# A new annealed emission order for an attention and gated-FFN kernel, with the rms factor of batches 4 and 5 moved to ScalarE

## The chip, the cores and the metric

The kernel runs on one core of a Trainium2 chip. The metric is the device time of one execution in microseconds (us). "Span" is the time from the first to the last instruction in the profile of one execution.

## What is computed

The inputs are q, k and v (8 batches, 8 heads, sequence 576, head dimension 64), g_norm (64), w_in (512 x 1024), conv_w (3 x 1024) and w_out (1024 x 512), all in float32.

```python
kv = einsum('bhsd,bhse->bhde', k, v)             # linear attention: no softmax
out = einsum('bhsd,bhde->bhse', q, kv)
rms = sqrt(mean(out * out, axis=-1) + 1e-06)
x = out / rms * g_norm                           # heads joined: (8, 576, 512)
h = maximum(x @ w_in, 0)                         # (8, 576, 1024)
c = conv_w[0] * h[s - 1] + conv_w[1] * h[s] + conv_w[2] * h[s + 1]
result = (h * sigmoid(c)) @ w_out                # (8, 576, 512)
```

## The kernel before

**Work.** The eight batches form five groups, (0), (1), (2, 3), (4, 5) and (6, 7), called g0 to g4. Each batch loads q, k and v as bf16 (`load`, L237, issued by GpSimd, 576 KB each; every name has two buffers, so the load of batch b waits until batch b - 2 has been read). TensorE makes kv (`kv_mm`, L378), transposes q (`tr_mm`, L428) and multiplies (`out_mm`, L351, tile `ot_ps`). ScalarE squares the product (`square`, L451), TensorE sums the squares (`ss_mm`, L505), and the factor 1 / rms comes in one of two ways. With `by_act`, ScalarE does Ln and Exp (`ln_exp`, L516 and L517), ahead of which L512 loads the table of these functions if a sigmoid ran last; the first sigmoid after it loads its own again (at L792 in this profile). Without it, `mean` (ScalarE, L521), `guess` (VectorE, L526) and `newton` (twelve GpSimd operations, L532 to L535) do the same. The factor is then spread over the partitions: g0 to g2 keep the product in SBUF (`keep`, L335) and spread with a matmul (`rb_mm`); g3 and g4 store the factor to DRAM (`scr`, L579) and read it back with eight broadcast transfers of 288 KB (`rb`, L585), both issued by SyncE in `scatter`, and form the product again (`out_again`). VectorE multiplies (`x_mul`, L640; `x_scale`, L646), which gives xT.

The FFN takes eight blocks of 128 features for each batch: `h_mm` (L744), relu (`h_out`, L755 on ScalarE or L757 on VectorE), the convolution with `tap` (L808), `edge` (GpSimd, L820) and `add` (L829, L831) on VectorE, or on TensorE for g0 (`conv_mm`, L783), sigmoid (L835, or L792 for g0), `gate` (L840), and `o_mm` (L696) for 128 rows of output at a time, `o_out` (L331 or L333) and `o_store` (SyncE, L710). The last 64 rows of two batches share one `tails_mm` (L883). `move` (L331 on ScalarE, L333 on VectorE) does all plain copies out of PSUM.

**Order.** No compiler schedules this. Every unit of work is an operation made by `plan.op`, numbered in the order of these calls. The list ORDER gives the order in which the operations are emitted, and so the order of each engine's own in-order queue. "101a" puts operation 101 on ScalarE, "20d" on VectorE, and "41*6" puts six fill matmuls, which compute nothing that is used, ahead of operation 41 to keep TensorE busy. Waits between engines follow from the data and from the buffers. The costs, `dma`, `lat` and `lead` that `plan.op` gets were used by a planner outside this file to find the list; at run time only the list counts.

Some numbers, in the list of before: 17, 34, 106, 208, 230, 368, 386, 522 and 540 are the kv products of batches 0 (in two parts) to 7. 205 and 206 load k and v of batch 3; 362 to 364 load k, v and q of batch 4, 365 to 367 of batch 5, 516 to 518 of batch 6, 519 to 521 of batch 7. 13 and 14 load the halves of w_in, 15 and 16 those of w_out. 404 sums the squares of g3, 405 to 407 are its `mean`, `guess` and `newton`, 408 its `scatter`, 410 its first `x_scale`; 558 to 562 are the same five for g4. 151 and 175 are the `edge` copies of g1, 291 and 323 those of g2. As g3 has one operation in place of three in the changed kernel, all numbers above 405 fall by two there: `ln_exp` of g3 is 405, its `scatter` 406, the loads of batches 6 and 7 are 514 to 519, their kv products 520 and 538.

The two ways to the factor, as they are put in the plan:

```python
if g.by_act:
    me = rs = plan.op("ACT", 0.97, ln_exp,
                      deps=[ss] + ([g.new_rs] if ts[0] else []))
...
else:
    me = plan.op("ACT", 0.5, mean, deps=[ss])
    g.new_rs = rs = plan.op("DVE", 0.3, guess, deps=[me])
    rs = plan.op("POOL", 11.5, newton, deps=[rs])
```

Of the kernel before, what the change touches and what calls it, by code (L numbers as in the profile page):

```python
# [25 lines left out]
def _patch_pnc_remap() -> None:  # L26
# [40 lines left out]

BY_ACT = (1, 1, 1, 0, 0)
Q_DMA = (0, 0, 0, 0, 0)
# [6 lines left out]
ORDER = """  # L76
    12 7 8 9 10 17*15 18d 19 29 105 20a 21*1 11 22 30d 31*1 23d 33a 34 35d 36 37a 24*1 25d 32 26*5
    28d 27 41*6 42 0 1 2 3 38 108*4 39 40d 113 43 45 109d 123 124a 4 103 44 104 114d 47 48 46 49 50
    106*2 107a 51*1 52 53 118 119a 110*2 54 112d 111 115 13 55 117a 204 56d 68 116 120 69a 122d 121
    14 225 125 210 126 64 211d 226d 127a 65a 5 59 60a 128 129 73 203 74d 66 67 215 202 77 78a 207 86  # L80
    87a 216a 130 131 132 70 133 71 134 135 136 208 209a 137 205 138 220 221d 75 76 79 80 212 214d
    222 232 233d 237 139 213 223 140a 242 82 238a 224d 83d 243a 6 147 72 217 218 219a 141 142a 143
    144a 149 247 364 370 371a 248a 169 84 85 206 81 374 375d 148 367 227 228 229a 230 88 89 170a 163
    231d 234 235 236a 249 250 90 164d 251d 378 379d 244 245 246d 239 240 363 388 362 145 146a 392
    389d 393d 366 151 400*2 252 57 253 58 150 152 156 401d 241d 61 382 383d 154 62 368 369a 167*4
    168a 155 153 165 166a 254 255 157 372 396 373 365 376 256 16 269 397a 270 386 267 268 377 387a
    261*2 262 63 380*4 381 15 394*3 395 175 259 260 402*2 403 390*3 391 398*2 171 174 384 385 399
    160 173 172 176 179 180 518 521 91 92a 93 158 177 178 100 101a 404 181 257 265 263 405 406 258
    264 266 159 183 161 97 98d 162 184 185 182 186 94 95a 516 517 277 271 542 524 275 102 543a 528
    525a 529a 199 272a 278a 276d 522 523a 273 274d 279 280a 281 200a 99 282a 287 288 289 285 286d  # L90
    407 283 284a 307 308a 532 533a 530 531 554 555a 315 316a 309 310a 305 306a 519 290 291 520 292
    296 294 293 295 297 550 551a 408 303 304a 319 534 535 540 541a 320 317 318a 322 311 312a 313
    314a 546 547d 321 323 324 328 526 552 527 553 548 536 537a 556 557 193 549 538 539 544 545 201
    409 194a 325 410 413 414 558 411 415 195 559 560 196 421 298 301 416 417 190 96 197a 299 191a
    326 192 300 412 422 418 327 329 187 188a 189 198 425 426a 423 424 433 330 419 420 302 434a 461
    333 462a 435 427 428d 436d 441 443 332 331 334 429 437 561 438a 430a 439 440a 431 432a 442 445
    459 469 470a 463 465 464a 466a 460a 471 457 458a 444 446 450 449 467 356 468a 472a 448 447 451
    562 357a 358 473 475 476 474 454 338 339a 340 477 478 480 479 482 344 345a 455 346 353 354a 355
    359 360a 567 563 481 571 335 564 572 568 452 453 336a 347 565 348a 569 575 483 484 485 486 349
    341 570 576 350 566 577 361 578 573 574 456 579 580a 605 487 587 488 627 628a 585 586a 590 606a  # L100
    342a 343 581 582a 583 584a 591 351a 607 608a 588 589 592 593 594 596 595 597 352 337 603 604a
    609 610a 615 492 611 493a 674 675a 494 601 498 499a 599 613 489 500 600 490a 491 631 632a 504
    633 598 629 614 612 616 618 620 617 619 621 623 602 634a 630a 653 654a 639 622 505a 506 501 635
    638 636 637 640 641 642 643 624 502a 625 651 652a 503 507 508a 644 645 647 626 649 648 509 665
    510 511a 512 513 666a 646 514a 515 657 655 656 658 660 689 659 661 662 495 650 667 668 669 670
    690a 691 671 663 664 496a 497 683 684a 685 686 677 676 678 679 680 672 673 681 682 687a 688 692
    693d 694 701 702a 703 707 708d 709 704 705d 706 698 699d 700 695 696a 697
"""
# [5 lines left out]
class Ring:  # L114


    def __init__(self, bufs):
        self.free = bufs
# [12 lines left out]
class Op:  # L131

    def __init__(self, at, group, engines, cost, fn, args, deps, need, dma, lat):
        self.at, self.group, self.engines, self.cost = at, group, engines, cost
        self.fn, self.args, self.dma, self.lat = fn, args, dma, lat
# [13 lines left out]
class Plan:  # L151
# [12 lines left out]

    def op(self, engines, cost, fn, *args, deps=(), need=(), dma=0.0, lat=0.0):
        engines = engines if isinstance(engines, tuple) else (engines,)
        cost = cost if isinstance(cost, tuple) else (cost,) * len(engines)
        o = Op(len(self.ops), self.group, engines, cost, fn, args, deps, need, dma, lat)
        self.ops.append(o)
        return o  # L170
# [18 lines left out]
def kernel(  # L189
# [112 lines left out]
    plan = Plan()  # L302
# [191 lines left out]
    def normalize(g, first, ts, sums):  # L494
# [58 lines left out]
        def x_view(bi, t):  # L553
# [4 lines left out]
                                deps=mine, need=g.need_rs)  # L558
        for sq in mine:
            Hold(ring("sq", 8), sq, [ss])  # L560
# [3 lines that stand above are left out]
            if ts[0] == 0:  # L564
                g.new_rs = rs
# [10 lines left out]
        if g.x_from == "dma":  # L576
            def scatter():
# [10 lines left out]

            g.scatter = sp = plan.op("SP", 8.3, scatter, deps=[rs], need=g.need_rb,
                                     dma=4.0 * g.G, lat=0.5)  # L590
            g.free_rs = [sp]
# [5 lines left out]
        else:  # L597
            sp = rs
# [72 lines left out]
    def ffn(g):  # L671
# [15 lines left out]
        for t0, n in units:  # L687
# [29 lines left out]
            cuts = 1 + (t0 + n - 1) // PS - t0 // PS  # L717
            so = plan.op("SP", 0.6 * cuts, o_store, deps=[ev], dma=0.65, lat=2.0)
            Hold(ONE, om, [ev])
# [153 lines left out]
    def tails(pair):  # L873
# [26 lines left out]
        st["op"] = ev = plan.op(EITHER, (0.6, 0.69), o_out, deps=[om])  # L900
        so = plan.op("SP", 1.2, o_store, deps=[ev], dma=0.65, lat=2.0)
        Hold(ONE, om, [ev])
# [59 lines left out]
    for half in range(2):  # L962
        loaded["w_in", half] = plan.op("POOL", 0.77, load_w_in, half, dma=2.7)
    w_out_done = [plan.op("POOL", 0.77, load_w_out, half, dma=2.75) for half in range(2)]

    for g in groups:
        g.by_act, g.by_dma, g.x_from, g.kv_twice = (c[g.n] for c in (BY_ACT, Q_DMA, X_FROM, KV_TWICE))
        for b in g.bs:
            for name, src in (("k", k), ("v", v), ("q", q)):
                if b > 0:  # L970
                    need = []
                    if b > 1:
                        w, wi = where[b - 2]
                        need = w.free_q[wi] if name == "q" else w.free_k[wi]
                    loaded[name, b, 0] = load_ops[name, b] = plan.op(
                        "POOL", 0.77, load, b, name, src, need=need, dma=2.95,
                        deps=[load_ops[name, b - 1]] if b > 1 else [])
# [54 lines left out]
```

## Time and profile before

The median of three runs is 214.91 us (214.76 to 218.9). The profiled execution took 213.96 us, its span is 212.2 us.

| engine | busy us | share of the span | instructions |
|---|---|---|---|
| PE (TensorE matmuls) | 187.7 | 88% | 1877 |
| PEld (weight loads) | 117.9 | 56% | 1877 |
| DVE (VectorE) | 153.5 | 72% | 283 |
| ACT (ScalarE) | 141.1 | 66% | 227 |
| POOL (GpSimd) | 50.5 | 24% | 73 |

| stretch, us | PE busy | DVE busy | ACT busy | POOL busy | clock of TensorE | GB/s |
|---|---|---|---|---|---|---|
| 40 to 50 | 9.97 | 7.25 | 8.92 | 3.80 | 1.00 | 152 |
| 70 to 80 | 10.00 | 9.63 | 9.20 | 6.04 | 1.00 | 151 |
| 80 to 90 | 6.68 | 3.38 | 3.92 | 7.95 | 0.94 | 184 |
| 90 to 100 | 10.00 | 6.05 | 6.74 | 0.91 | 0.89 | 213 |
| 100 to 110 | 3.66 | 5.56 | 2.96 | 0.00 | 0.79 | 167 |
| 110 to 120 | 9.31 | 5.67 | 7.83 | 0.22 | 0.87 | 2 |
| 140 to 150 | 10.00 | 9.72 | 6.97 | 0.86 | 1.00 | 216 |

A share of busy time averages over stretches with different limits, so the second table matters more than the first: in each stretch, ask which engine is full, and where none is, what they all wait for. In the trace, "waits" add up idle time of an engine by what ended it (engine, line, total us, times, longest). The "chain" goes back from the last instruction to what released it, again and again, and is printed in order of time (start, length, what, how many).

### The profile page before, as it was taken

How to read it: one execution, taken by the hardware profiler on the slowest of the kernel's cores; microseconds unless marked ns; L12 is line 12 of the kernel's file. 1: busy time of each engine (PE TensorE's matmuls, PEld its weight loads, DVE VectorE, ACT ScalarE, POOL GpSimd, SP SyncE). 2: the span in 40 equal slices, each digit the busy share in tenths (PEclk: the TensorE clock that was granted, in tenths of full speed). 3: DMA queues.
4: the chain of work that ended last, by engine and by line, in shares of the span. 5: the costliest groups of instructions: out<-in, count | busy, mean ns of one | idle time of the engine just before them, and what ended most of it. 6: DMA issues, size and time to landing. Idle time of an engine off the chain costs nothing.

```text
span 212.2 us, 4655 instructions
## 1 busy us (share of the span) xinstructions
PE 187.7 (88%) x1877; PEld 117.9 (56%) x1877; DVE 153.5 (72%) x283; ACT 141.1 (66%) x227; POOL 50.5 (24%) x73
## 2 busy tenths in 40 slices
PE   1988999999799999399259998999999999999992
PEld 1655567777575447277246446784446756654440
DVE  2047775778899995148904999999997999899430
ACT  2054679797898995257427898857688868896401
POOL 7714020205130649601000199401000000000000
PEclk9999999999999999889958999999999999999999
DMA  3999999999999599799920133089722243145654
GB/s 54 200 202 204 205 205 204 169 196 141 205 205 205 75 216 248 122 209 226 234 47 0 44 93 114 29 182 218 203 73 73 68 130 100 50 112 161 166 143 114
DMA packets 31593, 31.01 MB, mean 146 GB/s; under 512 B 2108, under 2 KB 26964, under 8 KB 31572
## 3 DMA queue, kind: packets, MB, share of 16 engines
q0 software_dynamic: 20976, 16.25, 50.5%
q1 hardware_dynamic: 10596, 14.47, 26.9%
q8 instruction: 14, 0.23, 0.4%
q14 instruction: 7, 0.06, 0.1%
HBM read 37.24 MB, written 9.73 MB: 221 GB/s over the span
## 4 chain that ended last, share of the span: by engine, by line
PE 55%; DMA 23%; DVE 11%; ACT 4%; issue 3%; POOL 2%; SPq 0%; DVEq 0%; ACTq 0%; POOLq 0%
PE h_ps L744 25%; PE o_ps L696 18%; DMA v_sb<-in_v_dram 13%; DMA k_sb<-in_k_dram 4%; DMA q_sb<-in_q_dram 4%; PE kv_ps L378 3%; DMA out_dram<-o_sb 3%; PE c_ps L783 2%; DVE xT L646 2%; PE qT_ps L428 2%; DVE o L335 2%; DVE conv L831 2%; PE ot_ps L351 2%; ACT sq L451 1%; DVE conv L829 1%
## 5 line engine op out<-in xcount | busy, mean ns | idle before, releaser
L744 PE MATMUL h_ps<-xT,w_in_sb 128*128 128x288 bf16 x512 | 69.6, 292 | 1.8 <-DVE o L335 0.7
L696 PE MATMUL o_ps<-w_out_sb,h 128*128 128x512 bf16 x272 | 61.2, 379 | 0.1
L744 PEld LDWEIGHTS <-w_in_sb 128*128 128x128 bf16 x512 | 50.0, 100 | 17.8 <-issue 3.0
L755 ACT ACTIVATE h<-h_ps 128x576 bf16<-128x576 f32 x55 | 34.9, 653 | 14.7 <-PE h_ps L744 13.2
L696 PEld LDWEIGHTS <-h 128*128 128x128 bf16 x272 | 26.0, 98 | 30.8 <-issue 1.5
L808 DVE TENSOR_SCALAR tap<-h,cw_rel 128x576 bf16<-128x576 bf16 (+1 forms) x80 | 31.7, 440 | 10.8 <-ACT h L755 9.9
L835 ACT ACTIVATE conv<-conv,cw_rel 128x576 bf16<-128x576 bf16 (+1 forms) x40 | 37.0, 959 | 1.9 <-DVE conv L831 1.9
L331 ACT ACTIVATE o_sb<-o_ps 128x512 f32<-128x512 f32 x31 | 18.5, 597 | 17.8 <-PE o_ps L696 12.8
L820 POOL COPY conv<-h 128x4 bf16<-128x4 bf16 (+3 forms) x12 | 3.8, 320 | 98.4 <-ACT h L755 76.2
L451 ACT ACTIVATE sq<-ot_ps 128x576 bf16<-128x576 f32 x32 | 20.0, 655 | 4.6 <-DVE o L335 3.1
L840 DVE TENSOR_TENSOR h<-h,conv 128x1152 bf16<-128x1152 bf16 (+3 forms) x16 | 22.4, 1402 | 0.5 <-ACT conv L835 0.5
L831 DVE TENSOR_TENSOR conv<-conv,tap 128x1152 bf16<-128x1152 bf16 (+11 forms) x36 | 21.5, 652 | 1.0
L829 DVE TENSOR_TENSOR conv<-h,tap 128x1152 bf16<-128x1152 bf16 (+11 forms) x36 | 20.4, 621 | 0.4
L378 PE MATMUL kv_ps<-v_sb,k_sb 96*64 96x64 bf16 x432 | 10.6, 210 | 10.2 <-DMA v_sb<-in_v_dram 9.7
L331 ACT ACTIVATE qT<-qT_ps 128x576 bf16<-128x576 bf16 x17 | 10.8, 654 | 12.4 <-PE qT_ps L428 12.4
L331 ACT ACTIVATE kv_sb<-kv_ps 64x256 bf16<-64x256 f32 x24 | 9.1, 377 | 12.7 <-PE kv_ps L378 12.3
L378 PEld LDWEIGHTS <-k_sb 96*64 96x64 bf16 x432 | 9.8, 125 | 12.1 <-issue 11.0
L757 DVE TENSOR_SCALAR h<-h_ps 128x576 bf16<-128x576 f32 x9 | 6.7, 755 | 11.0 <-PE h_ps L744 8.4
L237 POOL DMA_DIRECT2D q_sb<-in_q_dram x9 | 6.8, 759 | 32.2 <-PE qT_ps L428 31.4
L351 PE MATMUL ot_ps<-qT,kv_sb 64*64 64x288 bf16 x192 | 12.9, 300 | 1.6 <-DVE h L757 0.6
L428 PE MATMUL qT_ps<-ident,q_sb 96*128 96x96 bf16 x192 | 12.8, 206 | 0.3 <-DMA q_sb<-in_q_dram 0.3
L646 DVE SCALAR_TENSOR_TENSOR xT<-ot_ps,g_sb,rb 128x576 bf16<-128x576 f32 x16 | 12.2, 808 | 1.1 <-PE ot_ps L351 1.1
(72 smaller groups left out, 170.4 us busy)
## 6 DMA issues: line engine op xcount, KB each, us to landing
out_dram<-o_sb SPq DMA_DIRECT2D x24, 192.0 KB, 2.3
rb<-scr SPq DMA_DIRECT2D x16, 288.0 KB, 8.0
q_sb<-in_q_dram POOLq DMA_DIRECT2D x7, 576.0 KB, 10.0
k_sb<-in_k_dram POOLq DMA_DIRECT2D x7, 576.0 KB, 13.0
v_sb<-in_v_dram POOLq DMA_DIRECT2D x7, 576.0 KB, 12.1
out_dram<-o_sb SPq DMA_DIRECT2D x24, 128.0 KB, 2.4
out_dram<-o_sb SPq DMA_DIRECT2D x24, 64.0 KB, 2.0
w_in_sb<-in_moe_w_in_dram POOLq DMA_DIRECT2D x2, 512.0 KB, 15.6
```

Of the source, the lines that this page charges most:

```text
L331: nc.scalar.activation(dst, src, AX.Copy, scale=1.0 if scale is None else scale)
L351: nc.tensor.matmul(ps[i * D:(i + 1) * D, e, :HS], g.kv[bi][es, t, i, :], g.qT[bi][es, 2 * t + i, :], start=True, stop=True)
L378: nc.tensor.matmul(ps[half * D:(half + 1) * D, hp, i * (halves - 1), :], k_sb[:, h, r * D:(r + 1) * D], v_sb[:, h, r * D:(r + 1) * D], sta ...
L451: nc.scalar.activation(g.sq[bi, t], ust["ps"][:, :, :HS], AX.Square)
L696: nc.tensor.matmul(st["ps"][:n, :], g.h[:, f, t0:t0 + n], w_out_sb[:, f, :], start=(f == 0), stop=(f == n_ff - 1))
L744: nc.tensor.matmul(ps[:, e, :HS], w_in_sb[:, t, f * P:(f + 1) * P], g.xT[:, t, at:at + HS], start=(t == 0), stop=(t == n_hd - 1))
L755: nc.scalar.activation(dst, st["ps"][:, :, :HS], AX.Relu)
L808: eng.tensor_scalar_mul(cst["t"][:, f - f0, :], g.h[:, f, lo:lo + T], cw_rel[:, j, f:f + 1])
L829: nc.vector.tensor_add(c[:, :, here], h[:, :, here], t[:, :, there])
L831: nc.vector.tensor_add(c[:, :, there], c[:, :, there], t[:, :, here])
L835: nc.scalar.activation(cst["c"][:, f - f0, :], cst["c"][:, f - f0, :], AX.Sigmoid, scale=cw_rel[:, 1, f:f + 1])
L840: nc.vector.tensor_mul(hs, hs, cst["c"])
```

## The change

Group g3 (batches 4 and 5) gets its factor from ScalarE by Ln and Exp (`BY_ACT[3]`), so that GpSimd's `newton` is left to g4 alone. The planner's view of the DMA queues is altered: output stores and the spreading transfers occupy the queues for longer (1.2 for 0.65, and 5.3 for 4.0 per batch), and loads have a lead before their data moves. With these numbers the list was annealed anew. For the execution, only the list and `BY_ACT` count.

```diff
-BY_ACT = (1, 1, 1, 0, 0)
+BY_ACT = (1, 1, 1, 1, 0)
...
 ORDER = """
-    12 7 8 9 10 17*15 18d 19 29 105 20a 21*1 11 22 30d 31*1 23d 33a 34 35d 36 37a 24*1 25d 32 26*5
-    28d 27 41*6 42 0 1 2 3 38 108*4 39 40d 113 43 45 109d 123 124a 4 103 44 104 114d 47 48 46 49 50
-    106*2 107a 51*1 52 53 118 119a 110*2 54 112d 111 115 13 55 117a 204 56d 68 116 120 69a 122d 121
-    14 225 125 210 126 64 211d 226d 127a 65a 5 59 60a 128 129 73 203 74d 66 67 215 202 77 78a 207 86
-    87a 216a 130 131 132 70 133 71 134 135 136 208 209a 137 205 138 220 221d 75 76 79 80 212 214d
-    222 232 233d 237 139 213 223 140a 242 82 238a 224d 83d 243a 6 147 72 217 218 219a 141 142a 143
-    144a 149 247 364 370 371a 248a 169 84 85 206 81 374 375d 148 367 227 228 229a 230 88 89 170a 163
-    231d 234 235 236a 249 250 90 164d 251d 378 379d 244 245 246d 239 240 363 388 362 145 146a 392
-    389d 393d 366 151 400*2 252 57 253 58 150 152 156 401d 241d 61 382 383d 154 62 368 369a 167*4
-    168a 155 153 165 166a 254 255 157 372 396 373 365 376 256 16 269 397a 270 386 267 268 377 387a
-    261*2 262 63 380*4 381 15 394*3 395 175 259 260 402*2 403 390*3 391 398*2 171 174 384 385 399
-    160 173 172 176 179 180 518 521 91 92a 93 158 177 178 100 101a 404 181 257 265 263 405 406 258
-    264 266 159 183 161 97 98d 162 184 185 182 186 94 95a 516 517 277 271 542 524 275 102 543a 528
-    525a 529a 199 272a 278a 276d 522 523a 273 274d 279 280a 281 200a 99 282a 287 288 289 285 286d
-    407 283 284a 307 308a 532 533a 530 531 554 555a 315 316a 309 310a 305 306a 519 290 291 520 292
-    296 294 293 295 297 550 551a 408 303 304a 319 534 535 540 541a 320 317 318a 322 311 312a 313
-    314a 546 547d 321 323 324 328 526 552 527 553 548 536 537a 556 557 193 549 538 539 544 545 201
-    409 194a 325 410 413 414 558 411 415 195 559 560 196 421 298 301 416 417 190 96 197a 299 191a
-    326 192 300 412 422 418 327 329 187 188a 189 198 425 426a 423 424 433 330 419 420 302 434a 461
-    333 462a 435 427 428d 436d 441 443 332 331 334 429 437 561 438a 430a 439 440a 431 432a 442 445
-    459 469 470a 463 465 464a 466a 460a 471 457 458a 444 446 450 449 467 356 468a 472a 448 447 451
-    562 357a 358 473 475 476 474 454 338 339a 340 477 478 480 479 482 344 345a 455 346 353 354a 355
-    359 360a 567 563 481 571 335 564 572 568 452 453 336a 347 565 348a 569 575 483 484 485 486 349
-    341 570 576 350 566 577 361 578 573 574 456 579 580a 605 487 587 488 627 628a 585 586a 590 606a
-    342a 343 581 582a 583 584a 591 351a 607 608a 588 589 592 593 594 596 595 597 352 337 603 604a
-    609 610a 615 492 611 493a 674 675a 494 601 498 499a 599 613 489 500 600 490a 491 631 632a 504
-    633 598 629 614 612 616 618 620 617 619 621 623 602 634a 630a 653 654a 639 622 505a 506 501 635
-    638 636 637 640 641 642 643 624 502a 625 651 652a 503 507 508a 644 645 647 626 649 648 509 665
-    510 511a 512 513 666a 646 514a 515 657 655 656 658 660 689 659 661 662 495 650 667 668 669 670
-    690a 691 671 663 664 496a 497 683 684a 685 686 677 676 678 679 680 672 673 681 682 687a 688 692
-    693d 694 701 702a 703 707 708d 709 704 705d 706 698 699d 700 695 696a 697
+    0 105 11 104 8 10 12 1 2 7 17 18a 9 19 20d 29 30a 24 25d 26*5 27 21 22 6 34 35d 31 32 103 23a 36
+    37d 41*7 28d 38*3 40d 33d 4 42 43*6 44 108 109d 39 49 45 46 5 50 3 13 118*9 123 124a 51 53 119a
+    106 107a 54 204 47 110*5 111 113 114a 52 48 55 125 112d 56a 126 127d 14 203 202 68 69d 120 122d
+    210 211d 121 220 115 116 59 117d 60d 128 129 130 57 58 77 64 207 215 65a 78a 73 74a 221d 131 132
+    61 216d 62 225 226a 133 134 137 208 209a 138 206 135 82 136 83d 205 66 67 212 213 217 232 218
+    364 214d 219d 233d 247 139 140a 222 224d 223 248d 227 237 238a 143 144a 242 243d 147 149 63 141
+    75 228 142a 148 230 231d 362 79 229a 76 80 81 145 146a 363 15 234 249 250 236d 370 251a 70 239*4
+    16 235 71 150 151 367 240 152 371d 153 155 86*3 87a 378 382 366 383d 244 245 156 365 72 379d 167
+    252 168d 241d 253 254 374*2 375d 246a 84*3 85 163 164a 169 170a 88 165 154 89 255 157 158 166a
+    171 90 259 256 368 369a 173 260 172 160 91 265 175 266 372 373 92d 93 267 268 174 376 377 388
+    389a 384 385 396 397a 176 261*2 269 159 100 101a 161 179 516 515 270 262 177 257 386 380 97 387a
+    381 390 392 258 178 283 180 393a 391 514 181 185 98d 400 401d 263 394 395 182 183 162 522 523d
+    94 264 402 403 526 527d 184 519 398 271 399 95d 99 534 535a 520 521a 186 199 272d 284d 404 405
+    285 286d 200a 277 273 278d 274d 287 275 276d 540 548 279 541a 290 549a 280d 518 281 552 528 282a
+    529 517 536 537 538 539a 288 317 318a 309 313 314a 289 310a 291 292 294 293 96 311 312a 305 306a
+    295 296 544 545a 550 551 303 304a 102 297 406 315 316a 307 308a 323 546 553d 554 555 547 319 321
+    322 530 531a 190 191a 192 542 320 543 524 525 324 328 325 532 533 193 194a 407 408 409 410 556
+    557 558 559 413 411 414 196 415 412 416 417 421 422 300 298 301 187 299 419 418 201 420 423 437
+    424a 197a 438a 429 430a 431 425 432a 327 326 329 302 195 332 427 198 426a 439 428a 433 434a 441
+    440 435 560 436a 442 443 444 445 447 446 331 333 461 462a 465 459 466a 448 460a 330 334 463 455
+    456a 467 468a 469 188a 470a 457 458a 189 449 356 357a 358 464a 450 350 351a 352 453 359 360a 361
+    563 561 573 471 474 473 341 342a 343 472 475 476 562 574 564 452 335 336a 344 345a 353 354a 480
+    477 479 478 481 565 567 568 571 572 566 337 347 338 451 575 576 485 482 569 570 484 577 578a 454
+    603 604a 483 486 585 579 580a 586 583 584a 588 607 629 348a 630a 581 582a 601 602a 587 346 511
+    349 512a 608a 355 589 339a 590 591 592 593 605 606a 627 594 595 628a 599 597 625 609 663 496 631
+    340 610 613 612 611 614 616 618 664a 598 626a 632a 617 490 497a 615 596 491a 513 498 619 622 620
+    505 506a 507 600 633 634 492 636 635 649 651 508 652a 623 637 638 642 640 621 509a 510 641 502
+    650a 503a 639 643 647 645 646 624 499 500a 672 690 653 654 644 655 504 501 691a 692 656 658 657
+    659 673a 648 493 494a 495 487 665 666 660 667 668 669 661 488a 662 674 675 489 676 677 678 684
+    685a 670 671 679 681 682a 687 686 680 693 683 688a 689 694d 695 705 706a 707 696 697d 698 699
+    700d 701 702 703a 704
 """
...
-            g.scatter = sp = plan.op("SP", 8.3, scatter, deps=[rs], need=g.need_rb,
-                                     dma=4.0 * g.G, lat=0.5)
+            g.scatter = sp = plan.op("SP", 8.3, scatter, lead=2.5, deps=[rs], need=g.need_rb,
+                                     dma=5.3 * g.G, lat=1.0)
...
-            so = plan.op("SP", 0.6 * cuts, o_store, deps=[ev], dma=0.65, lat=2.0)
+            so = plan.op("SP", 0.6 * cuts, o_store, deps=[ev], dma=1.2, lat=1.5)
...
-        loaded["w_in", half] = plan.op("POOL", 0.77, load_w_in, half, dma=2.7)
+        loaded["w_in", half] = plan.op("POOL", 0.77, load_w_in, half, lead=1.8, dma=2.7, lat=0.5)
...
-                        "POOL", 0.77, load, b, name, src, need=need, dma=2.95,
+                        "POOL", 0.77, load, b, name, src, need=need, lead=1.8, dma=2.95, lat=0.5,
```

The tails' store and the loads of w_out get the same new numbers; `Op` and `Plan.op` take the new argument `lead`.

More of the change, by code (lines that the diff above doesn't have):

```diff
@@ L131, with __init__ @@
 class Op:
-    def __init__(self, at, group, engines, cost, fn, args, deps, need, dma, lat):
+    def __init__(self, at, group, engines, cost, fn, args, deps, need, lead, dma, lat):
         self.at, self.group, self.engines, self.cost = at, group, engines, cost
-        self.fn, self.args, self.dma, self.lat = fn, args, dma, lat
+        self.fn, self.args, self.lead, self.dma, self.lat = fn, args, lead, dma, lat
         self.kind = fn.__name__ if fn else ""
@@ L163, in __init__, with op @@
         self.ops, self.group = [], 0
-    def op(self, engines, cost, fn, *args, deps=(), need=(), dma=0.0, lat=0.0):
+    def op(self, engines, cost, fn, *args, deps=(), need=(), lead=None, dma=0.0, lat=0.0):
         engines = engines if isinstance(engines, tuple) else (engines,)
         cost = cost if isinstance(cost, tuple) else (cost,) * len(engines)
-        o = Op(len(self.ops), self.group, engines, cost, fn, args, deps, need, dma, lat)
+        o = Op(len(self.ops), self.group, engines, cost, fn, args, deps, need,
+               max(cost) if lead is None else lead, dma, lat)
         self.ops.append(o)
@@ L900, in tails @@
         st["op"] = ev = plan.op(EITHER, (0.6, 0.69), o_out, deps=[om])
-        so = plan.op("SP", 1.2, o_store, deps=[ev], dma=0.65, lat=2.0)
+        so = plan.op("SP", 1.2, o_store, deps=[ev], dma=1.2, lat=1.5)
         Hold(ONE, om, [ev])
@@ L962 @@
     for half in range(2):
-        loaded["w_in", half] = plan.op("POOL", 0.77, load_w_in, half, dma=2.7)
-    w_out_done = [plan.op("POOL", 0.77, load_w_out, half, dma=2.75) for half in range(2)]
+        loaded["w_in", half] = plan.op("POOL", 0.77, load_w_in, half, lead=1.8, dma=2.7, lat=0.5)
+    w_out_done = [plan.op("POOL", 0.77, load_w_out, half, lead=1.8, dma=2.75, lat=0.5) for half in range(2)]
     for g in groups:
```

## The prediction

> **What bounds the kernel now.** I read first the waits of TensorE, as it is the busiest engine, then the chain of waits in order of time, then GpSimd's timeline, then windows of 5 us. TensorE has one large kind of wait:
>
> ```profile
> PE kv_ps L378 <- DMA v_sb<-in_v_dram: 9.7, 2, 6.3
> ```
>
> The chain (start, length, what) says when, and what released the load:
>
> ```profile
> 72.79 15.61 DMA v_sb<-in_v_dram
> 88.40 0.14 issue
> 88.54 1.49 PE kv_ps L378 x42
> 90.03 6.07 PE h_ps L744 x40
> 96.10 0.02 issue
> 96.12 0.66 ACT h L755
> 96.78 0.05 issue
> 96.83 0.14 POOL conv L820
> 96.97 11.69 DMA v_sb<-in_v_dram
> 108.66 0.04 issue
> 108.70 1.57 PE kv_ps L378 x48
> 110.27 4.21 PE h_ps L744 x24
> ```
>
> These are the v loads of batches 6 and 7. The last one is issued only at 96.97, behind an `edge` copy on the in-order GpSimd queue. GpSimd's timeline shows what stood before that:
>
> ```profile
> 76.73 0.67 POOL L532 TENSOR_TENSOR tmp<-rs 128x288 f32<-128x288 f32 x1 [3.17 <-DVE rs L526]
> ...
> 86.90 0.79 POOL L535 TENSOR_TENSOR rs<-rs,tmp 128x288 f32<-128x288 f32 x1
> 87.79 0.84 POOL L237 DMA_DIRECT2D k_sb<-in_k_dram  x1
> ```
>
> So `newton` of batches 4 and 5 holds the k load of batch 7 back by 11.0 us. The windows (busy us of PE, PEld, DVE, ACT, POOL; clock; DMA) show that all engines pay, and the clock too:
>
> ```profile
> 85.00:90.00 5.00, 1.68 (x52) 1.43 (x50) 0.76 (x1) 1.19 (x2) 3.28 (x5) 0.87 0.76 121
> 105.00:110.00 5.00, 1.30 (x47) 1.30 (x47) 0.81 (x2) 0.00 (x0) 0.00 (x0) 0.58 0.58 96
> 110.00:115.00 5.00, 5.00 (x47) 3.44 (x42) 0.74 (x2) 3.29 (x7) 0.00 (x0) 0.74 0.01 3
> ```
>
> From 118 us on, TensorE is busy almost without a break to 208.1, and VectorE 9.0 to 9.9 of 10 us in most windows.
>
> **What the Trainium skill says.** TensorE: Matmul & The Clock Gate (What's actually happening): an idle stretch halves the clock until TensorE has been busy again. The trace agrees: after the waits, the clock reads 0.79 (90 to 95 us) and 0.74. ScalarE: Activation LUTs (What ACT_TABLE_LOAD costs): 1.28 us and a drain of 1.38 us per switch. The trace has 1.28 us, and the load at 57.40 starts right after an activation, so I use 1.28. DMA: Bandwidth & Descriptors (Issuing engines are not separate DMA queues): all queues run on the same 16 engines. The load of 15.6 us agrees: three other loads and six stores, issued from 74.08, ran beside it.
>
> **The change, part by part.** Pitches from the chain: h_mm 0.98 us, o_mm 1.73, tails 1.85, kv_mm 0.96, conv_mm 0.75, transposes 0.26, products 0.25, a fill matmul 0.12. I add these over the entries of each ORDER list; "P = 60" means that TensorE has 60 us of work up to there. Likewise D for VectorE and A for ScalarE, with means from the rows and from the timeline. The sums for the list of before are P 175.5, D 151.3, A 141.5, against 187.7, 153.5 and 141.1 busy, so D and A can be trusted; PE's busy time holds slow clock and overlaps besides.
>
> (1) *The two waits.* 9.7 us. In the new list, GpSimd has the loads of batches 6 and 7 one after the other, with no `newton` and no `edge` among them. Their last conditions are the kv products of batch 4 (P = 48.4) and the last q transpose of batch 5 (P = 59.3). Batch 7's kv products come at P = 74. TensorE's time minus P, the "offset", is about 16 there (below): q7 is issued at 75, and k7 is wanted at about 90. Three loads of 576 KB at the page's 205 GB/s take 8.6 us, with 2 us before the first bytes (my estimate from the shortest landing, 5.5 us for 432 KB), so they land at 86 to 88 even with a store of 256 KB or two between. From the other side: all 24 loads and 4 weights, 16.25 MB in q0, need 79 us at 205 GB/s plus 3 us of start plus 5 us for the four stores of batch 0: 87. Both are 2 to 4 us early. For batch 6 the same gives 76 landed against 80 wanted. I take both waits as gone; the bad end is one half left, 5 us.
>
> (2) *The slow clock after them.* Five h_mm take 6.07 instead of 4.90, three take 4.21 instead of 2.94, the two kv 1.49 and 1.57 instead of 0.96: 1.2 + 1.3 + 0.5 + 0.6 = 3.6 us, gone with the waits.
>
> (3) *rms factor by ScalarE.* Away: one `mean` (0.50), one `guess` on VectorE (0.30), one `newton` (76.73 to 87.69). Added: Ln and Exp (0.52 + 0.44) and, as sigmoids stand before and after it in the list, two table loads of 1.28. ScalarE pays 3.0 us more, in the stretch P = 60 to 91 where it has 22 us of work in 31. Hidden there. Queued behind it is the evacuation of the tails; TensorE has h_mm on other banks meanwhile. The scatter of batches 4 and 5 can start at 67 + 16 + 3 = 86, is spread by 100, and its first reader comes at P = 88.5, that is 105. Cost 0.
>
> (4) *The other loads.* Before, v of batch 3 stood behind q of batch 4, which waits for transposes: issued at 40.75, and the DMA moved only 152 GB/s in 40 to 50. Now it goes ahead of it. In the first 70 us the loads then arrive 3 us or more ahead of their readers. Worth 0 by itself, as TensorE waited under 1 us on loads there.
>
> (5) *Stretch P = 36 to 60.* ScalarE and VectorE bind it: before, D 27.4, A 26.1 and P 24.1 took 28.7 us (49.1 to 77.8), 1.048 times the largest. Now A 25.9, D 25.3, P 23.9: 27.1 us. Gain 1.6.
>
> (6) *Fills.* 60 become 49: P total 174.2. The 15 before the first kv products go, so these run at a cold clock; 72 of them took 1.8 us, and twice that is +1.8 at most. But the first h_mm needs w_in, whose first half, issued at 9.22 and 15.6 us to landing, comes at about 25 (h_mm began at 26.48). Cost 0.
>
> (7) *VectorE takes more over:* counting the letters, 18 qT (15), 12 keep (10), 11 h (9), 6 o_sb (5), 2 kv_sb (3): D total 155.3, +4.0. From P = 91.3 to 162.0 the new list has D 70.1 (71.1 on the busy scale of the trace) for P 70.7. Before, P 72.4 and D 70.4 took 73.6 us there. So VectorE binds as much as TensorE; I take 73.3, an offset of 2.6.
>
> **Ledger.** First h_mm ends at 27.5 (P = 15.6); 21.6 us as before to P = 36.1, so 49.1; 27.1 to P = 60: 76.2. Then 31.3 of TensorE work to P = 91.3, with 1.5 for small waits (my choice; the skeleton 118 to 208 lost 2.5 in 90): 109.0. Then 73.3: 182.3. Then 12.2 of TensorE to the end and the tail of 4.1 (208.1 to 212.2): span 198.6. The time is 1.8 to 2.7 above the span: 201.
>
> **Rivals.**
> A (0.57), the ledger: 201.
> B (0.10), VectorE keeps out of the way and the small waits vanish: 201 - 2.6 - 1.0 = 197.5. For it: TensorE is unbroken in 130 to 143. Against: D equals P.
> C (0.23), a new wait takes part of the gain: half a load wait (5 with its clock), or batches 6 and 7's scatter. Their `newton` starts at about 107.5 and took 13.5 us (121.3 to 134.8), then 2.3 for the store to `scr` and 8 to 12 for spreading: 131 to 135, where the first x_scale is wanted at about 134, in the stretch that VectorE binds. Up to 3. Gives 204 to 207.
> D (0.10), the loads were not what counts: VectorE keeps its 58.7 us of idle time (212.2 - 153.5) because each engine waits for others all along, and has 4 us more to do: 214.9 + 4.0 = 219, slower than before. For it: VectorE's share is 9 of 10 wherever loads don't hold it. Against: 85 to 90 and 105 to 115, where everything stands still at once.
>
> **Numbers.** 201.0. The range holds A, B and most of C, 8.5 in 10: 197.3 to 207.5. Faster by over 2% means below 210.6: A, B, C and a little less for unseen trouble, 0.88; D splits into 0.07 within 2% and 0.05 slower.
>
> **What would show it.** No wait of TensorE on v_sb over 1 us; k and v of batch 7 landed by 90; clock 1.00 from 80 to 120; two more ACT_TABLE_LOAD; no `newton` before 100; DVE above 9.3 of 10 in most windows after 110; TensorE's last matmul near 194.5. I am wrong if kv_ps still waits, if x_scale waits for the spreading, or if o_ps waits for stores.

## The result and the profile after

The changed kernel takes 205.3 us (median of four runs, 204.8 to 212.8) against 214.9 us of the kernel before on the same chip: a ratio of 0.955, 95% interval 0.951 to 0.959. The profiled execution has a span of 203.0 us against 212.2. That is faster, inside the range on record, and 4.3 us above the time named there. (Some executions of most kernels here are 2 to 9 us longer, with a lower clock in the records; the ratios leave these out, the medians do not, and the profiles of e1 and e8 below are of such executions.)

Line numbers in the changed kernel are two higher than before. The same wait of TensorE on loads, in its list of waits, is now only the start of the kernel (at 9.0 us); one load wait of under 1 us stands where two of 3.4 and 6.3 stood, and two lines are new in weight:

```profile
ACT o_sb L333 <- DMA out_dram<-o_sb: 3.0, 1, 3.0
PE kv_ps L380 <- DMA v_sb<-in_v_dram: 2.7, 1, 2.7
PE o_ps L698 <- ACT o_sb L333: 2.0, 1, 2.0
PE kv_ps L380 <- DMA k_sb<-in_k_dram: 0.7, 1, 0.7
```

GpSimd's timeline (start, length, line) shows the three loads of batch 7 behind each other, with no `newton` among them. The time in brackets is the wait of q for the transposes of batch 5:

```profile
78.46 0.77 POOL L239 DMA_DIRECT2D q_sb<-in_q_dram  x1 [9.02 <-PE qT_ps L430]
79.23 0.77 POOL L239 DMA_DIRECT2D v_sb<-in_v_dram  x1
79.99 0.77 POOL L239 DMA_DIRECT2D k_sb<-in_k_dram  x1
```

The windows in which everything stood still before are full, at full clock (PE, PEld, DVE, ACT, POOL busy; clock; DMA share; GB/s):

```profile
85.00:90.00 5.00, 5.00 (x54) 3.57 (x51) 3.43 (x5) 3.38 (x6) 0.00 (x0) 1.00 1.19 221
105.00:110.00 5.00, 5.00 (x59) 2.08 (x56) 4.81 (x8) 4.33 (x9) 0.18 (x1) 1.00 0.50 110
110.00:115.00 5.00, 4.95 (x39) 2.27 (x37) 4.76 (x8) 4.97 (x6) 3.79 (x6) 1.00 0.31 84
```

The chain of waits, where it passes batch 7:

```profile
79.99 14.24 DMA k_sb<-in_k_dram
94.23 0.04 issue
94.27 1.04 PE kv_ps L380 x48
95.31 5.01 PE h_ps L746 x40
```

The 40 matmuls (five h_mm) took 6.07 us before, in the cold clock. So the two waits and the slow clock behind them are gone. Set against the ledger on record, mark by mark:

| mark | on record | measured | the stretch up to it, against the record |
|---|---|---|---|
| first h_mm ends (P = 15.6) | 27.5 | 29.0 | +1.5 |
| P = 36.1 | 49.1 | 52.5 | +1.9 |
| P = 60 | 76.2 | 78.8 | -0.8 |
| P = 91.3 | 109.0 | 111.9 | +0.3 |
| P = 162 (12.2 before TensorE's end at 198.9) | 182.3 | 186.7 | +1.5 |
| span | 198.6 | 203.0 | 0 |

Three stretches hold what is missing: the start, the one after it and the last long one. (The 0 of the last row says only that TensorE's work from P = 162 on and the 4.1 us after its end are as they were put.) The chain of the first 30 us is TensorE alone, from its first kv products on:

```profile
9.00 2.13 PE kv_ps L380 x72
11.13 1.79 PE qT_ps L430 x18
12.92 1.20 PE ot_ps L343 x5
...
18.61 1.16 PE rb_ps L624 x4
...
24.53 0.96 PE kv_ps L380 x48
...
27.98 1.00 PE h_ps L746 x8
```

And from 121 to 142 us the chain goes from `newton` of g4 through the store of its factor, the spreading transfers (issued by SyncE, L587) and one output store behind them to the copy out of PSUM that needs this store's buffer, and so to o_mm:

```profile
121.15 2.98 POOL rs L537
124.15 1.75 DMA scr<-rs
...
126.64 4.49 DMA rb<-scr
131.13 0.58 ACT o_sb L333
131.72 0.34 SPq L712
...
132.10 9.15 DMA out_dram<-o_sb
...
141.35 0.61 ACT o_sb L333
...
142.00 1.46 PE o_ps L698 x6
```

That store took 9.15 us; the stores of 192 KB in this stretch have a median of 2.3 us. From 142.0 to its end TensorE is on the chain alone.

### The profile page after: what moved, and what is told of

Its sections match the earlier page's. It is cut to its first block, busy times and chain, and to the rows that moved or that the text cites. A ratio compares the mean times of both kernels' runs of the same rounds, so it can differ in the third digit from the quotient of the medians.

```text
span 203.0 us, 4614 instructions
## 1 busy us (share of the span) xinstructions
PE 183.1 (90%) x1854; PEld 115.8 (57%) x1866; DVE 156.7 (77%) x289; ACT 139.2 (69%) x223; POOL 39.9 (20%) x61
## 4 chain that ended last, share of the span: by engine, by line
PE 52%; DMA 18%; issue 10%; POOL 9%; ACT 5%; DVE 4%; SPq 0%; POOLq 0%; ACTq 0%; DVEq 0%
PE o_ps L698 19%; PE h_ps L746 16%; DMA k_sb<-in_k_dram 7%; DMA out_dram<-o_sb 5%; DMA v_sb<-in_v_dram 3%; PE kv_ps L380 3%; PE qT_ps L430 3%; POOL rs L537 2%; PE rb_ps L624 2%; DMA rb<-scr 2%; PE c_ps L785 2%; ACT sq L453 2%; DVE o L337 2%; PE ot_ps L343 1%; POOL tmp L534 1%
## 5 line engine op out<-in xcount | busy, mean ns | idle before, releaser
L746 PE MATMUL h_ps<-xT,w_in_sb 128*128 128x288 bf16 x512 | 67.4, 286 | 2.2 <-ACT h L757 1.8
L698 PE MATMUL o_ps<-w_out_sb,h 128*128 128x512 bf16 x260 | 60.3, 379 | 2.6 <-ACT o_sb L333 2.0
L746 PEld LDWEIGHTS <-w_in_sb 128*128 128x128 bf16 x512 | 48.9, 98 | 16.5 <-issue 2.9
L757 ACT ACTIVATE h<-h_ps 128x576 bf16<-128x576 f32 x53 | 33.3, 650 | 9.1 <-PE h_ps L746 8.7
L333 ACT ACTIVATE o_sb<-o_ps 128x512 f32<-128x512 f32 x30 | 17.8, 593 | 19.8 <-PE o_ps L698 10.3
L822 POOL COPY conv<-h 128x4 bf16<-128x4 bf16 (+3 forms) x12 | 3.3, 278 | 102.4 <-ACT h L757 71.9
L333 ACT ACTIVATE kv_sb<-kv_ps 64x256 bf16<-64x256 f32 (+1 forms) x25 | 9.6, 383 | 12.2 <-PE kv_ps L380 11.8
L648 DVE SCALAR_TENSOR_TENSOR xT<-ot_ps,g_sb,rb 128x576 bf16<-128x576 f32 x16 | 12.2, 811 | 3.0 <-PE ot_ps L353 2.7
L335 DVE COPY qT<-qT_ps 128x576 bf16<-128x576 bf16 x18 | 8.1, 453 | 8.0 <-PE qT_ps L430 8.0
L642 DVE TENSOR_TENSOR xT<-o,rb_ps 128x576 bf16<-128x576 f32 x15 | 11.0, 750 | 3.7 <-PE rb_ps L627 2.3
L337 DVE TENSOR_SCALAR o<-ot_ps,g_sb 128x576 f32<-128x576 f32 x12 | 9.6, 813 | 4.9 <-ACT sq L453 4.1
L380 PE MATMUL kv_ps<-v_sb,k_sb 96*64 96x64 bf16 x432 | 9.9, 204 | 3.4 <-DMA v_sb<-in_v_dram 2.7
```

What stands on the lines that cost most here:

```text
L333: nc.scalar.activation(dst, src, AX.Copy, scale=1.0 if scale is None else scale)
L380: nc.tensor.matmul(ps[half * D:(half + 1) * D, hp, i * (halves - 1), :], k_sb[:, h, r * D:(r + 1) * D], v_sb[:, h, r * D:(r + 1) * D], sta ...
L698: nc.tensor.matmul(st["ps"][:n, :], g.h[:, f, t0:t0 + n], w_out_sb[:, f, :], start=(f == 0), stop=(f == n_ff - 1))
L746: nc.tensor.matmul(ps[:, e, :HS], w_in_sb[:, t, f * P:(f + 1) * P], g.xT[:, t, at:at + HS], start=(t == 0), stop=(t == n_hd - 1))
L757: nc.scalar.activation(dst, st["ps"][:, :, :HS], AX.Relu)
```

## The experiments

Each run is compared with the kernel before on the same chip. "After" is the changed kernel; e1, e2 and e9 start from the list of before, the others from the list of after. Each result is the median, the span of the profiled execution and the ratio to the kernel before.

| run | median us | span us | ratio | 95% interval |
|---|---|---|---|---|
| after | 205.3 | 203.0 | 0.955 | 0.951 to 0.959 |
| after, once more | 207.3 | 205.2 | 0.962 | 0.957 to 0.967 |
| e1_kv7_early | 206.4 | 208.7 | 0.953 | 0.944 to 0.963 |
| e2_loads_early | 203.9 | 203.5 | 0.942 | 0.931 to 0.953 |
| e3_newton_ahead | 224.4 | 222.6 | 1.039 | 1.030 to 1.048 |
| e4_newton_behind | 206.4 | 205.1 | 0.955 | 0.946 to 0.964 |
| e5_first_fills | 205.4 | 202.0 | 0.956 | 0.952 to 0.960 |
| e6_four_out | 204.6 | 202.5 | 0.952 | 0.949 to 0.956 |
| e7_g4_by_act | 202.2 | 201.1 | 0.941 | 0.938 to 0.944 |
| e8_three_cures | 203.6 | 202.1 | 0.940 | 0.935 to 0.944 |
| e11_kv7_first | 201.7 | 199.3 | 0.939 | 0.934 to 0.944 |
| e10_taps_twice | 206.4 | 206.0 | 0.959 | 0.955 to 0.964 |
| e9_old_list_cured | 207.7 | 206.7 | 0.960 | 0.954 to 0.967 |

### Is it the loads? One part alone, in the list of before

The theory: the place of the loads of batches 6 and 7 on GpSimd's queue is what counts, and the rest of the new list little. The rival: VectorE and the old order hold the kernel above 210 anyway. First only k and v of batch 7 (519, 520) go ahead of `newton`:

```diff
-516 517 277 271
+516 517 519 520 277 271
...
-306a 519 290 291 520 292
+306a 290 291 292
```

> The kernel before, with one edit: the k and v loads of batch 7 stand right behind the v load of batch 6 on GpSimd's queue, ahead of newton and of the edge copy. Theory 1 (the gain of the change is the load waits and the slow clock after them): the second wait (6.3 us) and its clock (1.3 + 0.6) go, the first stays: 214.9 - 8.2 = 206.7. Theory 2 (VectorE and the order of everything else set the time, the waits only stand where slack is): under 3 us gained, 212 or more.

206.4 us. The wait of batch 7 is gone, that of batch 6 remains:

```profile
PE kv_ps L378 <- DMA v_sb<-in_v_dram: 3.5, 1, 3.5
```

Then q of batch 7, which waits for transposes, is also put behind k and v of batch 6, and the first transposes of batch 7 (542, 543) later:

```diff
-518 521 91
+518 91
...
-516 517 277 271 542 524 275 102 543a 528
+516 517 521 519 520 277 271 524 275 102 528
...
-530 531
+530 542 543a 531
...
-306a 519 290 291 520 292
+306a 290 291 292
```

> The kernel before, with all six loads of batches 6 and 7 in a row in the order q6, k6, v6, q7, k7, v7, ahead of newton, and the first q transpose of batch 7 put later, since its load is later. Nothing else of the new list, and newton of batches 4 and 5 still on GpSimd. Theory 1: both waits and all the slow clock go, 214.9 - 13.3 = 201.6, which would be less than the changed kernel's 205.3. Theory 2: 210 or more.

203.9 us, ratio 0.942. The forecast of 201.6 is missed by 2.3; the profiled execution has a dip of the clock at 20 to 30 us (last section), and the two executions with a mean clock of 0.998 took 202.6. The last load is issued at 76.97, where it was 96.97, and `newton` follows:

```profile
76.97 0.78 POOL L237 DMA_DIRECT2D v_sb<-in_v_dram  x1
79.36 0.67 POOL L532 TENSOR_TENSOR tmp<-rs 128x288 f32<-128x288 f32 x1 [1.61 <-DVE rs L526]
```

After that TensorE's list has no wait on these loads over 0.5 us. The rival falls: five entries moved in the old list are worth the whole change in time. By the ratios this kernel is no slower than after, whose list is new throughout.

### The factor of g3: a wait put back, and the factor alone

In the list of after, `newton` of g3 returns, once ahead of v and k of batch 7 and once behind them (407 is `newton`; numbers above 405 are again two higher):

```diff
-BY_ACT = (1, 1, 1, 1, 0)
+BY_ACT = (1, 1, 1, 0, 0)
...
-404 405 285 286d
+404 405 406 407 285 286d
```

> The changed kernel with the rms factor of batches 4 and 5 by newton on GpSimd again, emitted right behind its guess, so ahead of the v and k loads of batch 7. If these loads are what counts: newton starts at about 87 and ends at 98, the two loads land at about 106 instead of 94, TensorE waits 12 us more at their kv products, with 2 to 3 us of slow clock: 217 to 220. If moving the loads away from newton did not matter: 205 to 208. But if both loads are handed over before newton because TensorE's sums of squares come after them, newton is behind them anyway, and the time is that of the next run.

224.4 us, 4% slower than even the kernel before, and 4 us above the range forecast: k lands at 111, not at 106, and the wait is 17, not 12. The issue of k moves from 79.99 to 99.64, and TensorE's largest wait, its chain and its window read:

```profile
PE kv_ps L380 <- DMA k_sb<-in_k_dram: 17.1, 1, 17.1
```

```profile
99.64 11.42 DMA k_sb<-in_k_dram
111.10 1.62 PE kv_ps L380 x48
```

```profile
100.00:110.00 10.00, 0.00 (x0) 0.00 (x0) 4.43 (x7) 0.00 (x0) 1.01 (x2) 0.50 1.14 202
```

So the new list takes a load behind `newton` worse than the old one did: by these waits TensorE comes to the kv products of batch 7 at 94.0 us and goes on at 111.1, where in the kernel before it came at 102.4 and went on at 108.7. What the Trainium skill says in TensorE: Matmul & The Clock Gate (What's actually happening), on which the prediction drew, is met here too: after an idle stretch the clock is 0.50 in this window, and the 48 matmuls behind it take 1.62 us instead of 1.04.

```diff
-517 536
+519 407 538
```

> The changed kernel with newton of batches 4 and 5 on GpSimd again, but behind all loads of batch 7. The part of ScalarE alone: its 0.96 us and two table loads of 1.28 go, newton ends at about 98 in place of Ln and Exp at 88, the scatter lands at about 111 in place of 101, where the first x_scale came at 108.9, and the first edge copy of batches 2 and 3 waits from 93.7 to 98. Theory: 0 to 3 us slower, 205.3 to 208.3. If ScalarE's share is worth as much as the loads, 210 or more.

206.4 us, ratio 0.955, the ratio of after. The factor is late now, and TensorE waits for the product that VectorE scales with it:

```profile
PE ot_ps L353 <- DVE xT L648: 3.6, 3, 3.0
```

The span is 2.1 us longer than that of after, but the ratios (each to 0.4 to 1.0%) do not show it. It is a balance: against the 3.6 us of this wait, the wait of o_ps for ScalarE (2.0 us in after) is not in TensorE's list of waits, and that for relus is 0.6 instead of 1.8 us. What Ln and Exp on ScalarE bring on their own is between nothing and 2 us as far as these runs tell. What counts is that no `newton` stands ahead of the loads; this kernel and e2 have that with `newton` of g3 still on GpSimd.

### Where are the missing 4 us? Three cures in the list of after

First the fills ahead of the first kv products come back:

```diff
-17 18a
+17*15 18a
```

> The changed kernel with the fifteen fill matmuls put back ahead of the first kv products. The prediction held that taking them away costs nothing, as w_in lands at 25 us anyway; but TensorE was busy without a break from 9.0 to 28.98 and its first 72 kv products and 18 transposes took 2.0 us more than at full clock. If that chain set the start: first h_mm ends at about 27 in place of 28.98 and the time falls by 1 to 2 us, to 203.5 to 204.5. If what comes later has slack of that size: first h_mm earlier, the time within 0.4 of the changed kernel.

205.4 us, as the first run of after. Beside after, run again with it (207.3 us; its profile has a clock of 0.72 in 20 to 25), it is a little faster (0.956 to 0.962, the intervals overlap). The first h_mm ends at 28.1 us, not at the 27 forecast. The early kv products take 1.33 instead of 2.13 us and those of batch 2 begin at 39.12 instead of 39.98, so 0.9 us of the start comes back. At batch 7 half of it is gone again (93.80 instead of 94.27): k is the later one there. At the end about 1 us of span is left (202.0), and less than that can be told from the ratios.

> The changed kernel unaltered, on the same chip as the next three, so that differences of 1 to 2 us can be read: 205.

Then a fourth buffer for the output rows:

```diff
-outp = pool("outp", 3)
+outp = pool("outp", 4)
```

> The changed kernel with four output buffers in place of three. In its trace, a store took 9.15 us beside the spreading transfers of batches 6 and 7, ScalarE waited 3.0 us for the buffer and TensorE 2.0 for ScalarE, and from there to the end the chain is TensorE alone. If this wait sets the end: 2.0 us less, 203.2. If VectorE, which was busy without a break from 105 to 147, sets it: within 0.5 of the changed kernel.

204.6 us, ratio 0.952: clear of after, once more, on the same chip (0.962), but not of the first run of after (0.955). The wait for the store's buffer falls from 2.0 to 0.7 us. The span is only 0.5 us shorter (203.0 to 202.5), as batch 7's kv products began 0.8 us later in this execution (95.10 instead of 94.27):

```profile
PE o_ps L698 <- ACT o_sb L333: 0.7, 1, 0.7
```

From these products to the long run of 64 h_mm matmuls near 150 us, after takes 57.5 us (94.27 to 151.76) and this run 56.2 (to 151.32): the 1.3 us by which the wait fell come through in this stretch, so the buffer is part of it. Third, g4 gets its factor from ScalarE too, so that no `newton` is left and the spreading starts earlier (numbers above 559 fall by two):

```diff
-BY_ACT = (1, 1, 1, 1, 0)
+BY_ACT = (1, 1, 1, 1, 1)
...
-556 557 558 559 413
+556 557 413
```

> The changed kernel with the rms factor of batches 6 and 7 by ScalarE as well, so no newton at all; the spreading can start at about 117 in place of 125.9 and is over before the output products of batches 2 and 3 begin at 132. No table load is added, since Ln and Exp of batches 4 and 5 were the last functions. If the collision of stores and spreading costs the 2.0 us: the wait goes as in the run with four buffers, and VectorE loses its slow stretch beside newton (an add of 4.17 in place of 2.70) too: 202 to 203.3. If not: 204.5 to 205.5.

202.2 us, ratio 0.941 (0.938 to 0.944): clear of after. The wait of o_ps is gone. An add of VectorE that lay beside `newton` is also faster; first the timeline of VectorE in after, then in this run:

```profile
116.61 4.17 DVE L833 TENSOR_TENSOR conv<-conv,tap 128x2304 bf16<-128x2304 bf16 x3
```

```profile
117.97 2.70 DVE L833 TENSOR_TENSOR conv<-conv,tap 128x2304 bf16<-128x2304 bf16 x3
```

What TensorE feels of the slow add is its wait for relus, which stand behind a sigmoid that waits for this add (1.56 us at 120.88 in after); first in after, then in this run:

```profile
PE h_ps L746 <- ACT h L757: 1.8, 2, 1.1
```

```profile
PE h_ps L746 <- ACT h L757: 0.6, 1, 0.6
```

From the kv products of batch 7 to the long h_mm run, this run takes 53.9 us (95.88 to 149.82) where after took 57.5. So `newton` of g4 and what follows from it cost 3.6 us there. Of TensorE's waits, 2.0 for the store's buffer and 1.2 for relus are gone, together 3.2; the rest is not accounted for. The spreading starts only 3.7 us earlier (122.25 instead of 125.95, not at the 117 forecast), though the factor is done at 112.3: on SyncE's queue its store to DRAM is issued at 120.16, right behind four output stores issued from 111.11 to 120.12. The 1.6 us by which batch 7 begins later here are the first 30 us (first h_mm ended at 29.8 instead of 29.0) and a longer wait for k (1.5 instead of 0.7).

The edits of e5, e6 and e7 together, and then with v and k of batch 7 ahead of its q:

> The changed kernel with the three edits together: fifteen fills ahead of the first kv products, four output buffers, and the rms factor of batches 6 and 7 by ScalarE. The last alone gave 202.2. The fills gained 1.2 us at the first kv products of batch 2 and less than half of it at the end; the fourth buffer has nothing left to save. 201.2 to 202.2 if the fills' gain is used up by the wait for k of batch 7; 200.5 to 201 if it goes through.

```diff
-391 514 181
+391 514 518 517 181
...
-280d 518 281
+280d 281
...
-529 517 536
+529 536
```

> The kernel with the three edits, and besides the v and k loads of batch 7 ahead of its q load, which waits on GpSimd's queue until the last q transpose of batch 5 is done (9 us) and holds them back. TensorE still waited 0.7 to 1.5 us for this k. If that wait is what uses up the fills' gain: 0.7 to 1.5 us below the run with the three edits. If VectorE sets the time after it: under 0.4 below.

e8 has a ratio of 0.940, e11 one of 0.939, both as e7 within their intervals. The span of e11, 199.3 us, is the shortest of all runs; its k comes early, and q is the late one:

```profile
PE qT_ps L430 <- DMA q_sb<-in_q_dram: 0.9, 1, 0.9
```

e11 (201.7 us, 201.0 at best) has the lowest ratio, 6% under before and about 1.6% under after, though not told apart from e7 or e8. On record its comparison with the kernel before counts as unclear in spite of the interval, so the 6% rest more firmly on e7 (0.938 to 0.944). Most of the gain over after is e7's; what the fills, the buffer and the order of the loads add to it is not resolved.

### Does VectorE bind the last stretch?

Step (7) rests on it. In the list of e7, eight taps of g3 are computed twice, the second time with the same result, so the output is the same. VectorE has eight operations more (157.9 us busy instead of 154.0), and no other engine has anything more.

```diff
-eng.tensor_scalar_mul(
+for _ in range(2 if g.n == 3 and j == 0 else 1): eng.tensor_scalar_mul(
```

> The kernel with the factor of batches 6 and 7 by ScalarE (202.2), with the eight first taps of batches 4 and 5 computed twice on VectorE: 8 x 0.45 = 3.6 us more of VectorE in the stretch from 118 to 140, nothing else altered. If VectorE sets the time of that stretch, as the prediction has it: 2.7 to 3.6 us slower, 205 to 206. If TensorE does and VectorE has slack: under 1 us slower, below 203.2.

206.4 us, ratio 0.959 against 0.941: 1.8% of the time before, or 3.9 us, as much as VectorE got in work. The chain shows where, for the profiled execution. In e7 the long h_mm run is

```profile
149.82 7.95 PE h_ps L746 x64
```

and in e10

```profile
153.00 9.67 PE h_ps L746 x64
```

Batch 7's kv products begin 0.5 us later in e10 (96.36), so 2.7 of the 3.2 us arise between them and this point; VectorE's slack took up about 1.2 of the 3.9. Then 1.7 us more come from a low clock (0.83 in 150 to 160), behind waits of TensorE for VectorE's `xT` of 0.8 us and less. That these waits set off the low clock is not shown, and it is not in every execution: one with a mean clock of 1.000 took 205.6 us, still 3.4 more than e7. So VectorE has about 1 us of slack in this stretch and sets its time beyond that.

### The same cures in the old list

e2 with ScalarE's factor for g3 and g4 and the fourth buffer:

```diff
-BY_ACT = (1, 1, 1, 0, 0)
+BY_ACT = (1, 1, 1, 1, 1)
...
-outp = pool("outp", 3)
+outp = pool("outp", 4)
```

> The kernel before with its own list, the six loads of batches 6 and 7 early (203.9 alone, 202.6 in its fastest executions), no newton at all and four output buffers; of the new list nothing is used. If the new list's gain is only the loads and newton: as fast as the changed kernel with the three edits, 200 to 202. If the rest of the new list is worth something: 203 or more. The two table loads for batches 4 and 5 fall into 75 to 80 us, where ScalarE is full, and may cost 1 to 2 of it.

207.7 us, ratio 0.960: worse than e2 (0.942). In this list sigmoids stand on both sides of Ln and Exp, so that g3 and g4 cost two table loads each; in the list of after, g4 costs none (e7 has one at 112.30 where after has one at 110.19). ScalarE's timeline has

```profile
77.09 1.28 ACT L512 ACT_TABLE_LOAD   x1
...
79.38 1.28 ACT L835 ACT_TABLE_LOAD   x1
```

and again at 111.74 and 114.02. The second pair falls into a stretch in which ScalarE is the full engine and TensorE waits:

```profile
110.00:120.00 10.00, 7.46 (x67) 3.13 (x61) 9.01 (x14) 9.88 (x13) 0.00 (x0) 0.98 0.20 54
```

And the spreading of g3, issued from 87.86 where e2 has 95.41, now runs beside the last loads. The v load of batch 7 lands at 102.1, and TensorE waits 1.4 us for it:

```profile
75.63 26.45 DMA v_sb<-in_v_dram
PE o_ps L696 <- ACT o_sb L331: 2.0, 1, 2.0
```

The second line is of TensorE's waits, for a copy that ScalarE does behind sigmoids at 117.6. From batch 7's kv products to the long h_mm run (72 matmuls in this list), e9 takes 53.3 us and e2 50.3, which is 3.0 of the 3.2 us between their spans, and there the chain of e9 passes the two table loads at 111.74 and 114.02. Ahead of it, the dip of the clock in e2's profile hides what the late load costs. How the whole loss divides was not tried. The switch of engine is not a gain by itself: for g4 it paid in e7, where the list leaves ScalarE room, and with the same step for g3 and g4 this list lost.

## Why the prediction was right, and where its sum was off

**Steps (1) and (2), the waits and the clock: right.** The one wait left is 0.7 us on k, and the clock is 1.00 in every window of 5 us from 80 to 120. e1 and e2 bring each wait's share by moving loads alone, e3 brings a wait back. Inside step (1), the landing of k failed: "they land at 86 to 88" was 94.2, 14.24 us after the issue. Two terms were wrong. q was issued at 78.5, not 75, as the ledger itself was 2.6 us late there. And the estimate counted "a store of 256 KB or two", while SyncE issued six stores, 768 KB, from 77.7 to 84.7; in 80 to 86 the DMA moved 96, 172 and 161 GB/s instead of the 205 of the profile's page. With these two terms put right, the same sum gives 93. The slack of "2 to 4 us" and the lateness of everything else hid all but 0.7 us. The skill's statement in DMA: Bandwidth & Descriptors (Issuing engines are not separate DMA queues), that all queues share the same 16 engines, was cited and then used too lightly.

**Step (3), the factor by ScalarE: right within what can be told.** Cost 0: e4 has the ratio of after. Two more table loads came as forecast (85.69 and 110.19).

**Step (4), the other loads: not contradicted.** e2 has the whole gain without them; in the new list they were not tried alone.

**Step (5), P = 36 to 60: right in kind.** 26.3 us for 27.1.

**Step (6), the fills, "Cost 0": wrong.** The argument was that w_in lands at 25, so a slower start hides. But TensorE was never waiting for w_in: it is busy from 9.0 to 29.0 without a break, so every slower matmul pushes the first h_mm. It ended 1.5 us late. e5 gets 0.9 of this back at batch 2, of which half is left at batch 7; in the time of the kernel that is not resolved. The sum was at hand: P = 15.6 from 9.0 on ends at 24.6, so close to w_in that any slower matmul counts. It took 20.0 us instead, and 2.3 of the 4.4 us stand in the first three lines of the chain: 2.13 + 1.79 + 1.20 = 5.1 us where the pitches on record give 2.8. The allowance of "+1.8 at most" for a slow clock was made there and then left out of the ledger.

**"21.6 us as before to P = 36.1": mis-sized.** It took 23.5. TensorE is busy for 22.0 of them, against 21.2 of 21.6 before: 0.9 is more work between the two marks in this list, 1.0 more idle time, with waits of 0.6, 0.4 and 0.3 us on squares, products and relus. This was read in the trace and not tried.

**Step (7), VectorE in P = 91.3 to 162: the size nearly right, the cause half.** 74.8 us for "73.3". VectorE does bind, with about 1 us of slack (e10), and it is over 9.5 of 10 us in five of the seven windows from 110 to 180. But in e7, with no `newton`, the stretch takes only 71.2 (113.5 to 184.7), so the offset that is left to VectorE is 0.5, not 2.6. The 3.6 us above that in after go with g4's `newton`; by the waits that go with it, 1.2 are its collision with VectorE and 2.0 that of its spreading with the store. The two errors nearly cancel in the sum, which is luck.

**The rival that came true is C,** by its second half and not its first: batches 6 and 7's scatter. The time it gave (204 to 207) holds 205.3, in part by luck: of the 4.4 us above the ledger's span only 1.5 arise in the stretch that C speaks of, and 3.4 before 52.5 us, which no rival named. For the last stretch the prediction had the mechanism, and its last paragraph named "if o_ps waits for stores" as what would make it wrong. Two things in it were off. It looked for x_scale to wait for the spreading, but VectorE is unbroken from 105 to 146.7; the one that waited was the output store on the same queue and engines. And it gave C 0.23 against A's 0.57, and the ledger 0 us for it, though its own numbers put the spreading at 131 to 135 and it had counted it as late. **B fell** for this kernel: the stretch took 74.8 us for 70.7 of work, though in e7 it comes within 0.5. **D fell:** e2 gains all by loads alone, at the same VectorE work. Of the other signs, `newton` begins at 110.8 (not before 100) as forecast, and the last matmul ends at 198.9, not near 194.5, by the sum of the table.

## What to carry to other kernels

Before a move on an in-order queue is priced, list everything that stands on the queue until the next reader; five entries moved were worth as much here as a list annealed anew. When one large wait goes, price next the transfers that now meet: spreading and stores on one set of DMA engines cost here a wait of 2.0 us that the ledger had put at nothing. And an argument of the form "hidden behind a load" needs a look at whether the engine in question waits for that load at all.

## What the runs showed beside this

**A store beside spreading.** One output store took 9.15 us beside eight broadcast reads of 288 KB, where those of 192 KB nearby have a median of 2.3.

**VectorE beside GpSimd.** Three adds took 4.17 us beside `newton` and 2.70 without; `newton`'s own multiplications grew to 2.98. SBUF — State Buffer (Who interferes with whom) of the Trainium skill says that a VectorE instruction with two SBUF inputs contends with a GpSimd one that reads SBUF, and calls the ports that they share an exclusive lock. These rows agree in direction, and e7 shows that the add is fast when `newton` is away.

**A dip of the clock at 20 to 30 us.** It is in four of the fourteen profiles, of both lists: e1, e2, e8 and after, once more. In the last, TensorE had been busy without a break from 9.2 us on:

```profile
10.00:20.00 10.00, 10.00 (x146) 6.70 (x141) 5.35 (x16) 5.18 (x9) 3.22 (x5) 1.00 1.31 203
20.00:25.00 5.00, 5.00 (x34) 3.27 (x33) 4.84 (x6) 0.93 (x2) 0.00 (x0) 0.72 1.27 204
```

e2 had 0.82 and 0.50 in 20 to 30. The kv products of batch 2 come 2.0 us later than in after here, and in e2 and e1 2.4 and 4.1 us later than in before. So it is 2 to 4 us in an execution that has it. An idle stretch, which TensorE: Matmul & The Clock Gate (What's actually happening) gives as the cause of a slow clock, is not there in the first of the two. What sets it off stays open.
